# Attention and squared-ReLU feed-forward on one core: the first matrix product of chunks 3 to 6 by seven products, q of batches 2 to 7 loaded four tokens to a partition, the order of work searched anew

## The chip, the cores and the metric

The kernel runs on one core of a Trainium2 chip (trn2). The metric is device time in microseconds (us). The kernel before took 331.17 us, the median of three runs from 329.81 to 331.58. The engines are named as in the profile: PE multiplies matrices (PEld is its weight load), DVE, ACT and POOL work on vectors, SP and POOL issue most DMA transfers. PE writes its results to PSUM, eight banks of 512 fp32 numbers per partition; the others read them from there into SBUF.

## The reference

Causal attention with 16 extra "beacon" keys in front, for 8 batches of 8 heads, 576 tokens and 64 numbers per head, and then a feed-forward layer over all 4608 tokens:

```python
k_all = np.concatenate([beacon_k, k], axis=2)      # 592 keys, 5 tiles of up to 128
v_all = np.concatenate([beacon_v, v], axis=2)
scores = scale * np.matmul(q, k_all.transpose(0, 1, 3, 2))
scores = np.where(causal, -1e9, scores)            # beacons are always seen
a = softmax(scores)
attn = np.matmul(a, v_all)                         # [8, 8, 576, 64]
x = attn.transpose(0, 2, 1, 3).reshape(4608, 512)
h = x @ w_in                                       # 512 -> 2048, the first product
out = np.maximum(h, 0) ** 2 @ w_out                # 2048 -> 512, the second product
```

## The kernel before

**Order.** Every piece of work is a named operation on one engine, and a long word list (`SEQUENCE`, line 16) gives the order in which they are issued. `Order.run` (line 182) walks the list; `@A`, `@D`, `@P` after a name choose ACT, DVE or POOL where there is a choice. Each engine works its own instructions strictly in that order and waits by semaphores for what it needs. PSUM is handed out as two "strips" of two banks (scores) and four single banks `ps`.

**Attention.** Heads go in pairs, four pairs to a batch. `add_load` (line 370) reads 128 tokens of all heads into an fp32 staging tile: token on the partition, so each DMA row is one head of one token, 256 bytes. A cast (POOL, recorded at line 342 like every copy on DVE or POOL; line 340 on ACT) turns it to bf16 into `qb`/`kb`, of which there are two each, used in turn. `add_trans` (line 414, DMA at line 418) transposes a whole batch of q or k by DMA, so that `qT` and `kT` hold head dimension on partitions and tokens side by side. Batches 0 and 1 come in another way and are turned on PE (lines 474 and 476). `score_mm` (line 623, matmul at line 631) multiplies a 128-key tile by a stretch of q for each of the two heads of a pair; the two sit on partitions 0 to 63 and 64 to 127. A pair needs 1664 score columns, which are cut into the segments

```python
SEGS = [(0, 0, 240), (0, 368, 576), (1, 112, 576), (2, 240, 576), (3, 368, 576), (4, 496, 576), (0, 240, 368)]
```

(key tile, first token, last token). `add_stream` (line 663) lays the four pairs of a batch side by side, 13 banks of 512 columns, in visits of two or three. ACT takes the exponentials (line 729), DVE clips the diagonal tiles with a mask (line 750), PE multiplies by v (line 771, called av below), DVE divides (lines 788 and 790). The result goes transposed into `xT`, a ring of three batches (1728 tokens), by DMA (line 822) or PE (line 839).

In batch 0 the first 240 tokens are loaded two to a partition. There q stands in `qT` with all even tokens first and then all odd ones, 120 apart, and `score_mm` reads it with a step:

```python
rhs = qT[0][hp, pr, 0:parts_of[0][1][0]].rearrange("p (s n) -> p n s", s=ns)[:, t0 // ns:t1 // ns]
```

**Feed-forward.** 4608 tokens are nine chunks of 512. In chunks 0 to 6 the first product (`add_chunk`, line 1047, matmuls at line 1073) makes 16 tiles of 128 features, four matmuls of 512 columns each; where the ring wraps inside a chunk (chunks 3 and 6) each is cut in two. Per tile one pass over PSUM on ACT (line 1088) or DVE (line 1090) applies the ReLU, and one pass per two tiles squares in place (lines 1098, 1100).

The second product of chunks 2 to 8, and the first of chunks 7 and 8 (`BOTH = 7`), use seven products of half-size blocks in place of eight (Winograd's form). Sums of blocks are made beforehand: of `w_out` (line 882), of the squared g (line 1154, four per half chunk on DVE, in `sum_area`), of `w_in` (`add_a_sums`, line 890) and of x (line 930). In PSUM the products are added up in three chains: chain x takes products 1, 6, 7 and 4 one after the other into the same bank, and after each of the first three ACT or DVE copies the running sum out ("hold") before the next may be added; chains y (5, 3) and z (2) are read out with a held sum added ("plus", line 997). In chunks 7 and 8 (`add_first_both`, line 903, matmuls at line 950) chain x lies in the strips, which attention no longer needs, x is first copied ("pulled") into four contiguous blocks by POOL, and ReLU and squares are passes of their own (lines 1021 to 1029). `product` at line 1174 (matmuls at line 1182) is the second product's.

Of the kernel before, what the change touches and what calls it, by code (L numbers as in the profile page):

```python
# [12 lines left out]
BIG = 3.0e38  # L13
# [3 lines left out]
ident tri fldq0 fldk2 fldq1 bkl0 fldq2 fldk1 warm sld0k1.0 fldk0 sld0q1.0 fcq0 sld0k1.2 tp0.0.0q eq0.0.0@D sld0q1.2  # L17
fck2 tpg0.0.0q fck3 tp0.0.2k fcq1 ld0v0 bkc0 tp0.0.3k ek0.0.2@A ek0.0.3@D tpg0.0.2k tpb0 tpg0.0.3k tp0.0.1q ekb0
fcq3@A fcq2@D ld0v1 bkl1 eq0.0.1@A tp0.0.3q fck1 tpg0.0.1q tp0.0.2q ld0v2 eq0.0.3@A eq0.0.2@D qk3.0.0 tpg0.0.3q ld0v3
tpg0.0.2q tp0.0.1k tp0.1.0k exp3.0.0 fck0 ld0v4 qk2.0.0 ek0.0.1@D ek0.1.0@D tpg0.0.1k tp0.0.0k exp2.0.0 win0 qk1.0.0  # L20
mask3.0.0 tpg0.1.0k tp0.1.0q ek0.0.0@A mask2.0.0 exp1.0.0 qk0.0.0 tpg0.0.0k win2 tp0.1.2k eq0.1.0@A mask1.0.0 exp0.0.0
ek0.1.2@D qk0.1.0 tpg0.1.0q tp0.1.1q tpg0.1.2k win1 exp0.1.0 mask0.0.0 qk0.1.1 cast0v0@D tp0.1.1k exp0.1.1 eq0.1.1@D
qk0.1.2 mask0.1.1 win3 tpg0.1.1q tp0.1.2q ek0.1.1@A cast0v1@D exp0.1.2 eq0.1.2@D qk1.1.0 tpg0.1.1k bkc1 av0.0.0
tpg0.1.2q av1.0.0 sld1k0.0 exp1.1.0 mask0.1.0 tp0.1.3k norm0.0.0 qk2.1.0 cast0v2 tpb1 ek0.1.3@D qk1.1.1 exp2.1.0 ekb1
cast0v3 av2.0.0 norm1.0.0 tpg0.1.3k xtp0.0.0 exp1.1.1 tp0.1.3q xte0.0.0@D qk1.1.2 sld1q0.0 eq0.1.3@D xtp0.0.1 av3.0.0
exp1.1.2 norm2.0.0 tpg0.1.3q qk3.1.0 cast0v4 norm3.0.0 xtp0.0.2 exp3.1.0 sld1k0.2 qk2.1.1 mask1.1.0 av0.1.0 mask1.1.1
mask2.1.1 exp2.1.1 sld1q0.2 mask3.1.1 av1.1.0 xte0.0.1@A norm0.1.0 ld1v0 xte0.0.2@A xtp0.0.3 mask2.1.0 qk2.1.2
xte0.0.3@A norm1.1.0 xtp0.1.0 exp2.1.2 s1.0.1.0 xte0.1.0@D s1.0.3.0 relu0.1.0@D qk3.1.1 ld1v1 relu0.3.0@A s1.0.11.0
exp3.1.1 av2.1.0 relu0.11.0@D mask3.1.0 xtp0.1.1 s1.0.0.0 norm2.1.0 xte0.1.1@A s1.0.2.0 relu0.0.0@D qk3.1.2 ld1v2
relu0.2.0@A sq0.0.0@D xtp0.1.2 sq0.1.0@A s1.0.6.0 xte0.1.2@D exp3.1.2 s1.0.8.0 relu0.6.0@D s1.0.9.0 relu0.8.0@D  # L30
s1.0.10.0 relu0.9.0@A av3.1.0 sq0.4.0@D relu0.10.0@A ld1v3 sq0.5.0@D s1.0.12.0 norm3.1.0 s1.0.4.0 relu0.12.0@A
s1.0.5.0 relu0.4.0@A ld1v4 tp1.0.0k relu0.5.0@A xtp0.1.3 sq0.2.0@A ek1.0.0 s1.0.13.0 s1.0.14.0 xte0.1.3@A relu0.13.0@D
wout0 tpg1.0.0k tp1.0.0q relu0.14.0@A sq0.6.0@D s1.0.11.1 eq1.0.0@D tp1.0.1k relu0.11.1@A s1.0.8.1 wout1 tpg1.0.0q
ek1.0.1 tp1.0.1q relu0.8.1@A qk4.2 tpg1.0.1k eq1.0.1@D tp1.0.2k wout2 exp4.2.0.0.0 s1.0.15.1 tpg1.0.1q ek1.0.2
tp1.0.3q exp4.2.1.0.0 s1.0.12.1 wout3 tpg1.0.2k eq1.0.3@D s1.0.5.1 relu0.12.1@A mask4.0.0 qk4.4 tpg1.0.3q relu0.15.1@A
relu0.5.1@D cast1v0 s1.0.2.1 exp4.4.0.0.0 tp1.0.2q cast1v1 relu0.2.1@D s1.0.14.1 eq1.0.2@D exp4.4.1.0.0 cast1v2
s1.0.13.1 relu0.14.1@D s1.0.0.1 tpg1.0.2q relu0.13.1@A cast1v3 mask4.0.2 mask4.0.1 qk5.7 sq0.7.1@A sq0.6.1@D cast1v4
# [105 lines left out]
s2.8.1.0 sum8.4.1 sum8.2.0 s2.8.5.0 ev8.c1.0@A sum8.3.0 s2.8.1.1 sum8.4.0 s2.8.6.0 ev8.c1.1@A s2.8.5.1 ev8.u2.0@D  # L143
ev8.c11.None s2.8.7.0 st8.0.0.0 s2.8.6.1 st8.0.1.0 ev8.u3.0@A ev8.c22.0 s2.8.4.0 ev8.u2.1@A s2.8.7.1 ev8.c21.0@A
st8.1.0.0 s2.8.3.0 ev8.u3.1@A ev8.c22.1 s2.8.4.1 ev8.c12.0 st8.0.0.256 s2.8.3.1 ev8.c21.1@A st8.1.1.0 ev8.c12.1
st8.0.1.256
"""


# [1188 lines left out]
```

## Time and profile before

| | us |
|---|---|
| median of three runs | 331.17 (329.81 to 331.58) |
| span of the profiled execution, first to last instruction | 327.7 |
| busy PE / DVE / ACT / POOL | 315.9 / 231.9 / 225.7 / 101.1 |
| granted PE clock, mean | 1.000 |

The profile gives one execution. The span leaves out what lies before the first and after the last instruction: 331.17 − 327.7, some 3.5 us, if that execution was like the median run. A row of a group of instructions reads: line, engine, operation, output<-input with its shape, count | busy us, mean ns of one | idle us of the engine just before them, and what ended it. A row of the timeline reads: start, length in us, engine, line, operation, count. In a table of stretches each engine's busy us stand with the count of its instructions, then the granted PE clock, the DMA share and GB/s.

### The profile page before, as it was taken

Reading aid. Unit: us, or ns where it says so; the run is one execution under the profiler, and the core shown is the slowest. Engines: PE = TensorE matmul, PEld = TensorE weight load, DVE = VectorE, ACT = ScalarE, POOL = GpSimd, SP = SyncE. Lnnn points to the kernel's source line nnn. Section 1 sums busy time; section 2 is a strip of 40 time slices with the busy share of each in tenths; the row PEclk is TensorE's granted clock in tenths of the full one; section 3 lists DMA queues with packets and bytes.
Section 4 is the critical chain, followed back from the end, with each engine's and each line's share of the span. In section 5 each row is a group of like instructions: output and inputs, shape, how many; then the busy total and the mean of one; then the engine's idle time right before and its main releaser. Section 6 shows DMA issues by size and latency. Waiting matters only on the chain.

```text
span 327.7 us, 8732 instructions
## 1 busy us (share of the span) xinstructions
PE 315.9 (96%) x3582; PEld 227.6 (69%) x3582; DVE 231.9 (71%) x487; ACT 225.7 (69%) x332; POOL 101.1 (31%) x149
## 2 busy tenths in 40 slices
PE   2999999999999999999999999999999999999995
PEld 1478785544565558888866565776788788888884
DVE  3777886534655899587864788768865797897871
ACT  4867796458874984777766889767837664695931
POOL 9854713404532450424033403641100252000000
PEclk9999999999999999999999999999999999999999
DMA  8999998899999999999999998997913210110033
GB/s 159 220 205 215 206 169 170 168 214 204 205 177 201 240 219 171 178 244 230 180 138 215 221 181 204 202 207 156 225 23 130 46 28 2 69 61 0 2 148 111
DMA packets 145602, 51.98 MB, mean 159 GB/s; under 512 B 132506, under 2 KB 140570, under 8 KB 145562
## 3 DMA queue, kind: packets, MB, share of 16 engines
q1 hardware_dynamic: 135901, 42.32, 65.7%
q0 software_dynamic: 8512, 8.49, 15.4%
q10 hardware_dynamic: 1149, 0.62, 0.9%
q8 instruction: 28, 0.46, 0.6%
q14 instruction: 12, 0.10, 0.1%
HBM read 37.22 MB, written 9.44 MB: 142 GB/s over the span
## 4 chain that ended last, share of the span: by engine, by line
PE 85%; DMA 8%; SPq 1%; ACT 1%; POOL 1%; DVE 1%; issue 1%; ACTq 0%; POOLq 0%; DVEq 0%
PE ps L1073 26%; PE ps L1182 21%; PE ps L771 9%; PE ps L1123 8%; PE strip L631 6%; PE strip L950 4%; PE ps L950 3%; DMA stg<-in_q_dram 3%; PE strip L1182 2%; DMA kT<-qk_area 2%; PE ps L631 2%; DMA osb<-in_q_dram 2%; DMA stg<-in_v_dram 2%; PE ps L839 1%; SPq L822 1%; PE ps L474 1%
## 5 line engine op out<-in xcount | busy, mean ns | idle before, releaser
L1073 PE MATMUL ps<-xT,w_in 128*128 128x512 bf16 (+6 forms) x640 | 106.3, 315 | 0.6 <-ACT pt L729 0.6
L1073 PEld LDWEIGHTS <-w_in 128*128 128x128 bf16 x640 | 56.2, 98 | 34.8 <-issue 1.6
L729 ACT ACTIVATE pt<-strip 128x1024 bf16<-128x1024 f32 (+3 forms) x77 | 69.6, 955 | 7.8 <-PE strip L631 7.7
L1088 ACT ACTIVATE g<-ps 128x512 bf16<-128x512 f32 (+2 forms) x82 | 44.4, 551 | 20.1 <-PE ps L1073 17.2
L342 POOL CAST qk_area<-stg 128x512 bf16<-128x512 f32 (+2 forms) x60 | 39.9, 672 | 53.7 <-DMA stg<-in_k_dram 31.5
L342 POOL CAST vb<-stg 128x512 bf16<-128x512 f32 (+1 forms) x38 | 27.4, 728 | 83.6 <-DMA stg<-in_v_dram 69.4
L750 DVE TENSOR_TENSOR pt<-pt,tri 128x512 bf16<-128x512 bf16 (+1 forms) x93 | 37.8, 424 | 16.1 <-ACT pt L729 14.8
L1182 PEld LDWEIGHTS <-g 128*128 128x128 bf16 x448 | 42.9, 98 | 7.0 <-issue 0.8
L771 PEld LDWEIGHTS <-pt 128*128 128x128 bf16 x930 | 35.8, 100 | 7.0 <-issue 1.2
L771 PE MATMUL ps<-vb,pt 128*128 128x65 bf16 x930 | 38.4, 197 | 0.0
L1182 PE MATMUL ps<-w_out,g 128*128 128x256 bf16 x304 | 38.0, 273 | 0.0
L1090 DVE TENSOR_SCALAR g<-ps 128x512 bf16<-128x512 f32 (+2 forms) x46 | 27.9, 607 | 13.2 <-PE ps L1073 12.6
L1182 PEld LDWEIGHTS <-sum_area 128*128 128x128 bf16 x336 | 32.0, 98 | 5.5 <-issue 1.4
L790 DVE TENSOR_TENSOR xn<-ps,rcp 128x320 bf16<-128x320 f32 (+2 forms) x64 | 31.5, 491 | 2.2
L340 ACT COPY osb<-ps 128x512 f32<-128x512 f32 x26 | 15.2, 586 | 25.2 <-PE ps L1182 19.0
L1123 PE MATMUL ps<-w_out,g 128*128 128x512 bf16 x128 | 31.2, 379 | 0.0
L1100 DVE TENSOR_TENSOR g<-g 128x1024 bf16<-128x1024 bf16 (+2 forms) x35 | 23.4, 673 | 10.6 <-ACT g L1088 9.9
L631 PEld LDWEIGHTS <-kT 64*128 64x128 bf16 x618 | 20.0, 95 | 14.1 <-issue 10.3
L631 PE MATMUL strip<-qT,kT 64*128 64x128 bf16 (+14 forms) x500 | 29.5, 246 | 0.3 <-ACT qT L340 0.2
L1098 ACT ACTIVATE g<-g 128x1024 bf16<-128x1024 bf16 (+2 forms) x29 | 26.7, 941 | 3.0 <-DVE g L1090 2.0
L729 ACT ACTIVATE pt<-ps 128x512 bf16<-128x512 f32 x42 | 23.4, 599 | 5.7 <-PE ps L631 5.6
L1182 PE MATMUL ps<-w_sum,sum_area 128*128 128x256 bf16 x208 | 26.0, 273 | 0.0
(93 smaller groups left out, 357.7 us busy)
## 6 DMA issues: line engine op xcount, KB each, us to landing
out_dram<-osb SPq DMA_DIRECT2D x16, 512.0 KB, 3.8
stg<-in_q_dram SPq DMA_DIRECT2D x24, 256.0 KB, 4.6
stg<-in_k_dram SPq DMA_DIRECT2D x18, 256.0 KB, 5.1
stg<-in_v_dram SPq DMA_DIRECT2D x18, 256.0 KB, 4.6
w_in<-in_moe_w_in_dram POOLq DMA_DIRECT2D x4, 512.0 KB, 12.0
w_out<-in_moe_w_out_dram POOLq DMA_DIRECT2D x4, 512.0 KB, 10.9
stg<-in_v_dram POOLq DMA_DIRECT2D x6, 256.0 KB, 8.0
stg<-in_k_dram SPq DMA_DIRECT2D x6, 224.0 KB, 4.1
```

Source lines behind the costliest of these rows:

```text
L342: eng[e].tensor_copy(dst, src)
L631: nc.tensor.matmul(out, kT[b % 2][hp, pr, 128 * c:128 * c + 128], rhs, start=True, stop=True)
L729: nc.scalar.activation(out, in_, AF.Exp, bias=0.0, scale=scale)
L750: nc.vector.tensor_tensor(out=d, in0=d, in1=tri[0:rows, m0:m0 + m, 0:w][:, None].to_broadcast([rows, 2, m, w]), op=ALU.min)
L771: nc.tensor.matmul(a[:, at + (t - tl[0]) * (D + 1):at + (t - tl[0] + 1) * (D + 1)], P[0:rr, hj, o:o + 128], vb[b % 2][0:rr, c, 2 * pr + hj ...
L790: nc.vector.tensor_tensor(out=xn[b % 2].rearrange("p t (h d) -> p h t d", d=D)[:, h0:h0 + nh, tl[0]:tl[0] + nt], in0=a[:, :, :, 0:D], in1= ...
L1073: nc.tensor.matmul(h[:, lo - spans[0][0]:hi - spans[0][0]], w_in_sb[:, mc, ft * 128:(ft + 1) * 128], xT[:, mc, lo % RING:lo % RING + hi - lo],
L1088: nc.scalar.activation(dst, h, AF.Relu, bias=0.0, scale=1.0)
L1090: nc.vector.tensor_scalar(out=dst, in0=h, scalar1=0.0, scalar2=None, op0=ALU.max)
L1098: nc.scalar.activation(d, d, AF.Square, bias=0.0, scale=1.0)
L1123: nc.tensor.matmul(o, G[:, fc, ts * 128:(ts + 1) * 128], w_out_sb[:, fc, :], start=(fc == 0), stop=(fc == NFT - 1))
L1182: nc.tensor.matmul(o, lhs[:, f, t * 128:(t + 1) * 128], rhs[:, f], start=fresh and f == 0, stop=f == HF - 1, skip_group_check=True)
```

## The change

**First product.** `BOTH` becomes 3: chunks 3 to 8 all make the first product by seven products, in four units per chunk (4 of the 16 feature tiles each, two of the upper and two of the lower half), every chain in one `ps` bank. Blocks of x are no longer copied: products 1, 2, 3 and 7 read them in the ring, every second token (a step of two bf16 numbers); only the sums s1, s2 and s4 are separate tiles, and a fourth sum is written back into the ring. "Plus" becomes one custom DVE instruction that adds and clips at zero, so the ReLU has no pass of its own. Per chunk: 12 holds, 4 last passes of chain x, 12 plus, 8 squares, 4 sums of x.

**q.** For batches 2 to 7 a load takes two heads and 512 tokens, four tokens to a partition: DMA rows of 1024 bytes. After the transpose token 4n+s stands at 128s+n, and `score_mm` reads q with a step of 128 numbers (four tokens, then the next number). Tokens 512 to 575 are loaded as before, so a segment that reaches past 512 becomes two matmuls.

**Room and engines.** `qb` and `kb` are single; the other half of their area holds the sums of `w_in`. Casts may run on ACT, DVE or POOL, masks and sums of g on DVE or POOL (POOL masks with two `affine_select`). Two sums of g are made in place, after products 1 and 2. The word list is new throughout: 55 of 96 masks and 20 of 56 sums of g are on POOL, 19 casts of batches 0 to 7 on ACT, 20 on DVE (2 before) and 61 on POOL. Of the 96 holds and last passes of chain x, 70 are on ACT and 26 on DVE; the 72 plus are on DVE.

```diff
-    FAST, FAST_PE = 2, 0.9
-    BOTH = 7
-    NSTG, NPT, RB = 6, 3, 3
+    FAST, BOTH = 2, 3
+    NSTG, NPT, RB, NH = 6, 3, 3, 3
...
+        fours = x == "q" and c < HP
...
+            if fours:
+                return [queue.dma_start(out=st[0:rows].rearrange("p (u s) d -> p u s d", s=4),
+                                        in_=t[b, 2 * c:2 * c + 2, 0:4 * rows, :].rearrange("u (p s) d -> p u s d", s=4))]
...
         if x != "v":
-            if b < NPE + 2:
-                deps += [zero_ops[b]]
-            else:
-                deps += trans[b - 2, x]
-        engs = ("POOL", "DVE") if b == 0 and c <= 1 else ("POOL",)
+            deps += [zero_ops[b]] if b == NPE else trans[b - 1, x]
...
     def score_mm(b, pr, st, c, t0, t1, at):
...
+            if b >= NPE:
+                fours = qT[b % 2][hp, pr, 0:512].rearrange("p (s n) -> p n s", s=4)
+                parts = [(x, y, z) for x, y, z in ((t0, min(t1, 512), fours), (max(t0, 512), t1, None)) if x < y]
+            for x, y, view in parts:
+                out = st[hj][:, at + x - t0:at + y - t0]
+                if view is None:
+                    rhs = qT[b % 2][hp, pr, x:y]
+                else:
+                    ns = view.shape[2]
+                    out, rhs = out.rearrange("p (n s) -> p n s", s=ns), view[:, x // ns:y // ns]
+                nc.tensor.matmul(out, kT[b % 2][hp, pr, 128 * c:128 * c + 128], rhs, start=True, stop=True)
...
+        def in_ring(c, q):
+            return [xT[:, HM * c:HM * c + HM, lo % RING:lo % RING + hi - lo].rearrange("p m (i q) -> p m q i", q=2)[:, :, q]
+                    for lo, hi in spans]
...
+            product(2, "z", A[0, 1], b21, cuts, feeds + weights)
+            product(1, "x", A[0, 0], b11, cuts, feeds + weights)
+            hold("c1", 1)
+            plus("c11", "z", 2, block(0, 0), "c1", True)
+            product(5, "y", a_sum[1], [s[1]], one, a_ops[1] + x_ops[1])
+            product(6, "x", a_sum[2], [s[2]], one, a_ops[2] + x_ops[2] + ev["c1"])
+            hold("u2", 6)
+            product(7, "x", A[1, 0], b12, cuts, a_ops[3] + x_ops[3] + ev["u2"])
+            hold("u3", 7)
+            plus("c22", "y", 5, block(1, 1), "u3", False)
+            product(4, "x", A[1, 1], [s[4]], one, x_ops[4] + ev["u3"])
+            last("c21", 4, block(1, 0))
+            product(3, "y", a_sum[4], b22, cuts, a_ops[4] + ev["c22"])
+            plus("c12", "y", 3, block(0, 1), "u2", True)
```

591 lines of the change are left out of this document (296 added, 295 removed).

## The prediction

> **What bounds the kernel now.** I read the totals first, then who made PE wait, then two stretches: 140 to 260 us, where chunks 3 to 6 lie, and 280 to 300 us, where first products already go by seven.
>
> ```profile
> PE 315.9 (96%) x3582; PEld 227.6 (69%) x3582; DVE 231.9 (71%) x487; ACT 225.7 (69%) x332; POOL 101.1 (31%) x149
> ...
> PE ps L474 <- ACT qk_area L340: 5.8, 2, 5.3
> ...
> PE ps L1073 <- ACT pt L729: 0.6, 1, 0.6
> PE ps L631 <- DMA kT<-qk_area: 0.5, 1, 0.5
> ...
> 140.00:260.00 120.00, 118.87 (x1463) 87.06 (x1460) 87.66 (x183) 87.66 (x124) 30.68 (x45) 1.00 0.88 175
> 280.00:300.00 20.00, 20.00 (x186) 17.94 (x184) 18.13 (x34) 14.81 (x17) 0.00 (x0) 1.00 0.14 53
> ```
>
> PE works almost without a gap: 5.8 us of waiting at the start, then single waits of 0.6 and 0.5. ACT and DVE stand at 73% in the first stretch; in the second PE is full although DVE stands at 91%. So the time is PE's work, and each term below counts as it changes that work, or opens a gap in it.
>
> **What the seven products save.** A pair of rows gives a price: from one start to the next.
>
> ```profile
> 222.12 1.89 PE L1073 MATMUL ps<-xT,w_in 128*128 128x512 bf16 x8
> 223.85 1.04 PE L1182 MATMUL ps<-w_sum,sum_area 128*128 128x256 bf16 x8
> ...
> 255.62 7.15 PE L1073 MATMUL ps<-xT,w_in 128*128 128x384 bf16 x64
> 262.61 1.04 PE L1182 MATMUL ps<-w_out,g 128*128 128x256 bf16 x8
> ...
> 268.72 1.04 PE L950 MATMUL strip<-qk_area 128*128 128x256 bf16 x8
> 269.60 1.04 PE L1182 MATMUL ps<-w_sum,sum_area 128*128 128x256 bf16 x8
> ```
>
> Two plain tiles take 1.73 us, 0.865 each, so 13.84 for the 16 of chunk 4 or 5. Cut at the wrap, eight tiles take 6.99, so 13.98 for chunk 3 or 6; the cut costs 0.009 per tile, 2 ns per extra matmul. Eight matmuls of 256 columns take 0.88 at most (other such pairs 0.87, the value I use), and a chunk by seven products has 4 units x 7 products x 4 = 112 of them: 12.2 us. Chunks 3 and 6 read four of the products in two pieces, 64 more matmuls at 2 ns, 0.1. Saved: 2 x (13.84 − 12.2) + 2 x (13.98 − 12.3) = **6.6 us** (a quarter of a us either way by rounding).
>
> **What the step in scores costs.** The trace has such reads only in batch 0 (two tokens, 120 apart), each 240 + 128 = 368 columns for both heads side by side. Next to them stand plain score visits of 336 + 80 = 416 and 208 + 256 = 464 columns at the same time, and others later.
>
> ```profile
> 9.99 0.53 PE L631 MATMUL strip<-qT,kT 64*128 64x240 bf16 x4
> 10.45 0.38 PE L474 MATMUL ps<-ident,qk_area 120*128 120x120 bf16 x2
> ...
> 12.66 0.53 PE L631 MATMUL strip<-qT,kT 64*128 64x336 bf16 x4
> 13.12 0.49 PE L474 MATMUL ps<-ident,qk_area 112*64 112x112 bf16 x6
> ...
> 14.43 0.57 PE L631 MATMUL strip<-qT,kT 64*128 64x208 bf16 x4
> 14.93 0.49 PE L474 MATMUL ps<-ident,qk_area 112*64 112x112 bf16 x6
> ...
> 24.52 0.37 PE L631 MATMUL strip<-qT,kT 64*128 64x208 bf16 x4
> 24.83 0.32 PE L839 MATMUL ps<-ident,xn 128*128 128x128 bf16 x3
> ...
> 165.25 0.61 PE L631 MATMUL strip<-qT,kT 64*128 64x240 bf16 x10
> 165.80 1.92 PE L1182 MATMUL ps<-w_sum,sum_area 128*128 128x256 bf16 x16
> ...
> 176.13 0.62 PE L631 MATMUL strip<-qT,kT 64*128 64x48 bf16 x14
> 176.69 1.05 PE L1182 MATMUL ps<-w_out,sum_area 128*128 128x256 bf16 x8
> ...
> 8.00:10.00 2.00, 1.75 (x18) 0.94 (x18) 1.40 (x4) 1.17 (x3) 1.99 (x3) 1.00 1.58 193
> ```
>
> Early, 416 columns take 0.46 and 464 take 0.50: 0.83 ns per column, which would make 368 columns 0.42. With the step they took 0.46, and the other three such visits likewise: 0.04 more, about 0.1 ns per column, a pace near 0.93. From 24 us on PE runs twice as fast: 464 columns in 0.31, 1024 in 0.55, so 0.43 ns per column. (The granted clock reads 1.00 in the early stretch too; that halving is not in this column.) No stepped read falls in the fast part, so its price there is bounded. If the extra is a fixed start cost, it is 0.04 for each of 13 banks x 6 batches = 78: 3.1 us; if it shrinks with the pace, 1.6; if it is chance, 0. If instead a read that jumps at every number cannot be fed faster than about 0.93 ns, the early visits were almost fast enough not to show it, and in the fast part the pace stays there. Stepped columns: per pair 1664 less 64 for each of the five segments that end at 576, 1344; x 4 pairs x 6 batches = 32,256. With 0.91, the lower edge of what the rounding leaves, (0.91 − 0.43) x 32,256 = **15.5 us**; the upper edge, 0.97, gives 17.4. I take 15.5, the end to which the one stepped row points: an extra at half speed is what a limit in the feeding would look like, while chance would not come four times alike. So the range must reach from 0 to 17.4.
>
> [...]
>
> The cut at token 512 adds 5 x 4 x 6 = 120 pairs of matmuls. 14 matmuls for 1024 columns took 0.56 and 10 took 0.55, so 5 ns a pair: **0.6 us**.
>
> The first product's step of two numbers has no row. Ends: nothing, or the pace 0.91 for 4 products x 16 x 256 columns x 6 chunks = 98,304 columns, 47 us. I take 0, since successive numbers lie 4 bytes apart against 240 in the stepped row, nearer to the plain reads.
>
> **What ACT, DVE and POOL get.**
>
> ```profile
> L1088 ACT ACTIVATE g<-ps 128x512 bf16<-128x512 f32 x64 | 37.8, 599 | 16.9 <-PE ps L1073 14.5 <-DVE rcp L788 1.9
> L340 ACT COPY osb<-ps 128x512 f32<-128x512 f32 x26 | 15.2, 586 | 25.2 <-PE ps L1182 19.0 <-PE ps L1123 5.3 <-DMA out_dram<-osb 0.8
> ...
> L997 DVE TENSOR_TENSOR g<-ps,stg 128x512 bf16<-128x512 f32 x16 | 10.7, 684 | 3.4 <-PE ps L950 3.4
> L1154 DVE TENSOR_TENSOR g<-g 128x1024 bf16<-128x1024 bf16 x14 | 10.3, 740 | 0.0
> L750 DVE TENSOR_TENSOR pt<-pt,tri 128x512 bf16<-128x512 bf16 x62 | 29.5, 478 | 11.8 <-ACT pt L729 10.5 <-ACT pt L653 1.1
> ...
> L342 POOL CAST qk_area<-stg 128x512 bf16<-128x512 f32 x48 | 32.5, 680 | 43.8 <-DMA stg<-in_k_dram 24.6 <-DMA stg<-in_q_dram 18.8
> L327 POOL TENSOR_SCALAR_AFFINE_SELECT tri<-tri 128x128 bf16<-128x128 bf16 x4 | 1.0, 296 | 0.1
> ```
>
> A chunk had 16 passes over PSUM (0.60) and now has 28 of 0.59 to 0.68, and four sums of x (no row; at most the 0.74 of line 1154, which handles twice as many numbers without a step; I take the 0.68 of line 997, which has as many). That is 12 x 0.65 + 4 x 0.68 = 10.5 us a chunk, 42 in all. Casts add 37 x some 0.6 = 22. POOL takes away, over the whole run, 55 masks of some 0.42 (23 us) and 20 sums (15 us). Net 26 on two engines that had 175 of 240 in the first stretch: near 85%, below what DVE stood at from 280 to 300. I cost it at nothing, covered by PE's own work between a hold and the next product of its chain. Without that cover a hold (0.59) counts: 48 holds in chunks 3 to 6, 28 us. The order leaves two or three other PE pieces (1.2 to 1.3 us) between most of them, so I keep 0, with a rival below.
>
> **DMA and queues.** q's loads go from 24 x 1024 rows to 24 x 256.
>
> ```profile
> DMA  8999998899999999999999998997913210110033
> ...
> q1 hardware_dynamic: 135901, 42.32, 65.7%
> q0 software_dynamic: 8512, 8.49, 15.4%
> ```
>
> A packet took 0.657 x 16 x 327.7 / 135,901 = 25 ns on q1 (mostly 256 bytes), 95 on q0 (about 1 KB). So the loads' share goes from 24,576 x 25 / 16 = 39 us to between 10 (25 ns) and 37 (95 ns) for 6144. It lies beside PE, whose only wait for DMA was the 0.5 us, taken as gone, like the 0.6: **−1.1 us**. The single `qb` and `kb` make a batch's casts wait for the transposes before; behind a late cast stand the loads on SP, which need its staging tile, then the next scores. In the new order more than ten products lie between, so 0. The start is reordered too (the first transfer is the large one of q): bounded by the 5.8 us of waiting there, I take 0.
>
> **Sum.** 327.7 − 6.6 + 15.5 + 0.6 − 1.1 = 336.1 span, with 3.5 outside 339.6; rounded to **340 us**, against 331.2 for the median of the runs.
>
> **Rivals.** (a) *The step is free or nearly so*: PE really loses work. 331.2 − 6.6 + 0.6 − 1.1 + (0 to 3.1) = 324 to 327, with small gaps 326. For it: in batch 0 the extra is a tenth. This is the case on the other side: it decides at an extra of 0.22 ns per column (7.1 us), below which the kernel is faster. (b) *ACT and DVE now wait for loads*: POOL stood 43.8 us before 48 casts, 0.9 each; 37 casts now stand in the queues that also empty PSUM. If the step is free and 0.2 to 0.3 of each of these shows on PE, 7 to 11 us: 331 to 335. For it: `cast5q0` stands directly before a hold on ACT. Against: the loads are issued earlier. (c) *Both*: 340 + 9 = 349. (d) *The step of two numbers is slow too*: 340 + 47 = 387. Against it, 4 bytes.
>
> A sum on POOL reads two tiles from SBUF, as DVE's sums and squares do. [...]
>
> **How the numbers follow.** Chances: my case 0.50 (336 to 344), (a) 0.28, (b) 0.11, (c) 0.08, (d) 0.03. About 0.5%, 1.7 us, is what a measurement can tell from no change. Faster: (a) but for 0.02, and 0.02 of (b): 0.28. The same: 0.02 of (a), 0.05 of (b): 0.07. Slower: 0.65. The range runs from 324 to 346: it leaves out (d), most of (c) and the lowest edge of (a), some 0.15.
>
> **What would show it.** Right: a score visit of 1024 columns in batches 2 to 7 takes 0.9 to 1.0 us, not 0.55; a product of four matmuls in chunk 4 takes 0.44; PE busy grows by some 9 us with few waits. (a) shows as visits of 0.55 to 0.65; (b) as waits of PE for holds, with ACT idle on staging tiles; (d) as products of 0.8 us. I am wrong if the visits keep their length.

## The result, and the profile after

The changed kernel took 374.58 us in the median (371.87 to 376.88), the kernel before 331.27 beside it: a ratio of 1.132, 95% interval 1.126 to 1.139. The forecast was 340, the range ended at 346: the direction was foreseen, the size was not. Ratios and their intervals leave out executions in a slower state of the chip: one of six in the first kernel under "Order restored once" below and two of six in the third, whose medians and ranges hold them. The profiled execution is the slowest of its four, at 376.88 us; its span is 375.2 us against 327.7.

The page of the changed kernel: totals, granted clock over the span in 40 slices, and the largest DMA queue.

```profile
PE 356.6 (95%) x3988; PEld 254.1 (68%) x4002; DVE 253.1 (67%) x492; ACT 232.3 (62%) x353; POOL 149.7 (40%) x222
...
PEclk9999999999999999999999999989996999999999
...
q1 hardware_dynamic: 117469, 42.32, 52.4%
```

PE is busy 40.7 us longer and still fills 95%. So most of the 47.5 us is not waiting, it is matmuls that last longer. The rest shows in the waits of PE (engine, line, what it waited for: us in total, times, longest):

```profile
PE ps L826 <- DVE g L1048: 3.8, 1, 3.8
PE ps L826 <- DVE pt L806: 2.2, 1, 2.2
```

Before, no wait of PE behind the start was above 0.6. The two stalls on DVE, 3.8 and 2.2 us, are new. Which matmuls became longer is seen in the timeline (start, duration, engine, line; the price of a row is taken from its start to the next):

```profile
177.66 1.75 PE L681 MATMUL strip<-qT,kT 64*128 64x240 bf16 x14
179.34 0.72 PE L1219 MATMUL ps<-w_out,g 128*128 128x256 bf16 x5
...
211.65 0.62 PE L1010 MATMUL ps<-xT,w_in 128*128 128x256 bf16 x4
212.10 0.60 PE L1010 MATMUL ps<-spare,qk_area 128*128 128x256 bf16 x4
```

A visit of 14 score matmuls over 1024 columns, 896 of them read with the step, takes 1.68 us; before, a visit of 14 over as many columns took 0.56. The forecast had 0.9 to 1.0. A product of four matmuls with a step of two numbers takes 0.45, almost the 0.437 of one without.

A sum over the trace puts all in one table. Each matmul counts from its start to the start of the next one, but at most its own duration; what is left over is the gap. Groups by source line, us:

| | before | after | q read as stored | the same, x in halves | by tokens, x in halves |
|---|---|---|---|---|---|
| scores | 31.0 | 72.8 | 32.2 | 32.1 | 30.5 |
| first products, plain and by seven | 124.0 | 122.1 | 122.0 | 119.7 | 119.2 |
| second products | 115.4 | 114.8 | 114.0 | 115.4 | 115.5 |
| attention times v | 32.0 | 34.5 | 33.4 | 32.6 | 32.3 |
| gaps | 2.7 | 10.2 | 6.1 | 3.1 | 7.6 |

The last three columns are experiments below. In two of the traces, after and q read as stored, 14 plain matmuls have no record: that lowers both rows of products there, and about 1.1 us of their gaps lie at these places. Scores alone grew by 41.8, gaps by 7.5; the first products shrank by 1.9, where 6.6 were forecast.

The two stalls cost more than their gaps. Toward the end of each the granted clock fell to 0.50 and stayed there for some 3 and 7 us:

```profile
140.00:240.00 100.00, 99.85 (x1211) 74.31 (x1210) 71.01 (x132) 69.59 (x102) 47.49 (x82) 1.00 0.76 159
...
285.00:290.00 5.00, 4.82 (x52) 0.50 0.01 3
```

(The second line lists PE alone.) Behind the stall of 3.8 us two groups of av and one each of the second and the first product, from 285.18 to 289.49, took 4.31 us; the same four took 2.36 in the kernel "Sums off POOL" below, which hasn't this stall. Nowhere else in this execution was the clock under 0.9 for a whole us.

### The profile page after: what moved, and what is told of

It reads as the page before. It is cut to its first block, busy times and chain, and to the rows that moved or that the text cites. A ratio compares the mean times of both kernels' runs of the same rounds, so it can differ in the third digit from the quotient of the medians.

```text
span 375.2 us, 9752 instructions
## 1 busy us (share of the span) xinstructions
PE 356.6 (95%) x3988; PEld 254.1 (68%) x4002; DVE 253.1 (67%) x492; ACT 232.3 (62%) x353; POOL 149.7 (40%) x222
## 3 DMA queue, kind: packets, MB, share of 16 engines
q1 hardware_dynamic: 117469, 42.32, 52.4%
q0 software_dynamic: 8512, 8.49, 13.7%
## 4 chain that ended last, share of the span: by engine, by line
PE 87%; DVE 6%; issue 3%; DMA 2%; POOL 1%; ACT 0%; DVEq 0%; POOLq 0%
PE ps L1219 19%; PE ps L1010 18%; PE strip L681 14%; PE ps L1113 12%; PE ps L826 8%; PE ps L1162 7%; PE ps L681 4%; PE strip L1219 2%; DMA stg<-in_v_dram 2%; DVE g L1048 2%; DVE pt L806 1%; PE ps L894 1%; POOL qk_area L500 1%; DVE spare L986 1%; DVE xn L845 1%
## 5 line engine op out<-in xcount | busy, mean ns | idle before, releaser
L802 POOL TENSOR_SCALAR_AFFINE_SELECT pt<-pt 128x256 bf16<-128x256 bf16 (+1 forms) x92 | 36.6, 422 | 107.1 <-ACT pt L779 91.4
L1048 DVE CUSTOM_DVE_ANT_0 g<-ps,spare 128x512 bf16<-128x512 f32 x72 | 48.9, 687 | 23.5 <-PE ps L1010 18.1
L681 PE MATMUL strip<-qT,kT 64*128 64x128 bf16 (+14 forms) x652 | 61.8, 330 | 0.5 <-ACT qT L349 0.4
L349 ACT COPY spare<-ps 128x512 f32<-128x512 f32 x50 | 29.2, 588 | 35.1 <-PE ps L1010 34.3
L1113 PE MATMUL ps<-xT,w_in 128*128 128x512 bf16 (+2 forms) x250 | 45.6, 329 | 0.3
L1010 PE MATMUL ps<-xT,w_in 128*128 128x256 bf16 (+4 forms) x384 | 42.9, 250 | 0.5 <-DMA xT<-xn 0.5
L1074 ACT ACTIVATE g<-g 128x1024 bf16<-128x1024 bf16 x34 | 35.7, 1059 | 2.5 <-DVE g L1048 2.3
L1188 POOL TENSOR_TENSOR g<-g 128x1024 bf16<-128x1024 bf16 x14 | 31.0, 2225 | 15.6 <-DVE g L1188 11.2
L1010 PEld LDWEIGHTS <-qk_area 128*128 128x128 bf16 x320 | 27.7, 97 | 6.7 <-issue 1.5
L1010 PE MATMUL ps<-spare,qk_area 128*128 128x256 bf16 x192 | 28.7, 272 | 0.4 <-DVE spare L986 0.3
```

Of the source, the lines that this page charges most:

```text
L681: nc.tensor.matmul(out, kT[b % 2][hp, pr, 128 * c:128 * c + 128], rhs, start=True, stop=True)
L802: nc.gpsimd.affine_select(out=d[:, :, i], in_=d[:, :, i], compare_op=ALU.is_ge, fill=0.0, base=Nb if m0 + i == 0 else 0, pattern=[[0, 2], ...
L1010: nc.tensor.matmul(o[:, i * HT + at:i * HT + at + w], lhs[:, m, f * 128:(f + 1) * 128], part[:, m], start=fresh and i == 0 and at == 0 and ...
L1048: nc.vector._custom_dve(TENSOR_ADD_SAT, out=dst, in0=bank_of(chain), in1=held[keep[added].held[1]].rearrange("p (f t) -> p f t", f=2), s0= ...
L1074: nc.scalar.activation(both, both, AF.Square, bias=0.0, scale=1.0)
L1113: nc.tensor.matmul(h[:, lo - spans[0][0]:hi - spans[0][0]], w_in_sb[:, mc, ft * 128:(ft + 1) * 128], xT[:, mc, lo % RING:lo % RING + hi - lo],
```

## The experiments

Every variant of the whole kernel was timed beside the kernel before, on the same chip; its median there lay between 329.1 and 331.3. Between variants of different rounds, differences of 2 us or less are therefore read from the ratios.

**The step alone.** The kernel before, with q of batches 2 to 7 loaded by four and read by scores with the step; products and order as they were.

```diff
+        fours = x == "q" and c < HP and b >= NPE
...
+            if b >= NPE:
+                fours = qT[b % 2][hp, pr, 0:512].rearrange("p (s n) -> p n s", s=4)
+                parts = [(x, y, z) for x, y, z in ((t0, min(t1, 512), fours), (max(t0, 512), t1, None)) if x < y]
```

> The kernel before with the loads of four tokens and the stepped scores alone; seven products for chunks 7 and 8 only, order as before. Theory S: 331 + 43 = 374, within 4. Rival O: below 345.

It took 369.85 (369.63 to 370.3), ratio 1.119 (1.113 to 1.124), just under the 370 to 378 of theory S. The first line of its page:

```profile
PE 355.6 (97%) x3785; PEld 237.4 (65%) x3810; DVE 229.5 (62%) x487; ACT 228.5 (62%) x332; POOL 96.5 (26%) x149
```

PE is as busy as in the changed kernel, with almost no gaps. This one part makes nearly the whole slowdown.

**All but the step.** The changed kernel, with the loads by four and the cut at 512 kept, but q read in the order in which it is stored.

```diff
-                parts = [(x, y, z) for x, y, z in ((t0, min(t1, 512), fours), (max(t0, 512), t1, None)) if x < y]
+                parts = [(x, y, None) for x, y in ((t0, min(t1, 512)), (max(t0, 512), t1)) if x < y]
```

> The changed kernel with the loads of four tokens and the cut at token 512 kept, but q read as it is stored, without a step (the scores are of other tokens, so the output is not the reference's). Theory S: 324 to 331, and no slower than the run with q by tokens, since only the read is changed. Rival L (the loads of four tokens or their casts cost something): over 340 here while the run with q by tokens is near 330. Rival O: above 345 in both.

It took 329.54 (327.5 to 330.25), ratio 0.996 (0.993 to 0.998). The visit of 14 matmuls, and what follows it:

```profile
158.48 0.62 PE L681 MATMUL strip<-qT,kT 64*128 64x240 bf16 x14
159.03 3.67 PE L1219 MATMUL ps<-w_out,g 128*128 128x256 bf16 x32
```

The same 14 matmuls over the same columns take 0.55. The count of matmuls and the cut cost nothing that shows in this visit; the step costs 374.58 − 329.54 = 45 us in the new order. By the table 40.6 of it are the scores' own; this kernel also has neither of the two stalls.

**The loads alone, in the old order.** The step-alone kernel without its step, on the kernel before.

> The kernel before with q of batches 2 to 7 loaded four tokens to a partition and cut at 512, but read as stored, without a step (scores are of other tokens, the work is the same). Beside the kernel before at 331.3. If the loads and casts cost nothing by themselves, only the cut is left, 120 pairs of cut matmuls by some 5 ns: 331.3 to 332.3. If the loads by four ease a wait in the old order: under 330.5. If the casts of 128 rows by 1024 numbers hold up ScalarE or VectorE: over 333.

It took 329.59 (328.39 to 330.46), ratio 0.998 (0.996 to 1.000): a gain of some 0.8, in which the cost of the cut is contained. So the step costs 369.85 − 329.59 = 40.3 us in the old order. And against 329.54 above, the seven products, the new engines and the new order bring nothing in sum. That is a second question, taken up below.

**q by tokens.** The changed kernel with q loaded and read as before: no step, no cut.

```diff
-        fours = x == "q" and c < HP
+        fours = False
...
-            if b >= NPE:
+            if False:
```

> The changed kernel with q of batches 2 to 7 loaded and read as before (128 tokens to a load, no step, no cut at token 512); seven products and the new order stay. Theory S (the step in the scores costs nearly all of it: 30 visits, each 1.1 to 1.6 us longer than before): visits of 1024 columns take 0.55 us again and the time falls by some 43 us from 374.6, to 326 to 333. Rival O (the new order and the seven products cost most of it, by waits): the time stays above 345.

It took 333.91 (332.42 to 336.56), ratio 1.010 (1.007 to 1.014), just above the 326 to 333 of theory S. In the new order the loads by tokens cost 4.4 us against the loads by four: among PE's waits stands one of 2.4 us for the transposed k.

**The price of a read.** Matmuls alone, 16 for each pattern, one behind another. L47 reads 512 neighbouring numbers, L50 every second one, L53 every fourth, L59 every sixteenth; L62 takes 2 x 120 numbers from two places 120 apart in turn (the pattern of batch 0), L71 4 x 128 from four places in turn (the new scores), L74 4 x 120; L86 the same four places with two neighbours each time, L89 with four.

> Not the reference's computation: 16 matmuls each with the moving operand read in 16 patterns, the price of a column from start to start. If any jump at each number costs the same (theory J): 2 x 120, 2 x 128, 4 x 120, 4 x 136 and 4 x 128 all take about 1.7 ns per column, pairs half of that. If the distance matters (theory B: jumps of 256 bytes meet in one place of the memory): 4 x 128 and 2 x 128 take 1.7, while 2 x 120 and 4 x 136 take under 1.0. Steps of 2 and 4 numbers: 0.43 in both theories; 8 and 16 numbers (16 and 32 bytes) like a jump in J.

```profile
22.18 3.62 PE L47 MATMUL ps<-X,W 128*128 128x512 bf16 x15
25.63 3.78 PE L50 MATMUL ps<-X,W 128*128 128x512 bf16 x16
29.25 7.38 PE L53 MATMUL ps<-X,W 128*128 128x512 bf16 x16
36.45 2.88 PE L56 MATMUL ps<-X,W 128*128 128x512 bf16 x3
...
50.85 14.86 PE L59 MATMUL ps<-X,W 128*128 128x512 bf16 x16
65.54 3.84 PE L62 MATMUL ps<-X,W 128*128 128x240 bf16 x16
69.21 4.06 PE L65 MATMUL ps<-X,W 128*128 128x256 bf16 x16
...
80.86 13.99 PE L71 MATMUL ps<-X,W 128*128 128x512 bf16 x16
94.67 13.14 PE L74 MATMUL ps<-X,W 128*128 128x480 bf16 x16
...
149.14 7.18 PE L86 MATMUL ps<-X,W 128*128 128x512 bf16 x16
156.15 3.73 PE L89 MATMUL ps<-X,W 128*128 128x512 bf16 x16
159.72 3.62 PE L92 MATMUL ps<-X,W 128*128 128x512 bf16 x16
```

From start to start and per column (16 x 512 = 8192, for L62 3840): neighbours 0.42 ns (16 matmuls, of which the record holds 15), every second 0.44, every fourth 0.88, every sixteenth 1.79, four places in turn 1.69 (13.81 / 8192). With two neighbours at each place 0.86, with four 0.44, as good as plain. Two places in turn: 0.96 (3.67 / 3840). That the places lie 256 bytes apart doesn't matter: four places 240, 264 and 272 bytes apart cost 1.69 too. What counts is how many numbers are taken from a piece of 16 bytes before the read moves on: a step of eight numbers, 16 bytes, costs 1.76, and twice that step hardly more. Two expectations were missed: a step of four numbers should have cost 0.43, and two places as much as four, but two cost little more than half of four. And there lies the fault of the forecast: its pace of 0.93 per column from batch 0 is near what that pattern costs alone, but that is the pace for two tokens to a partition.

The granted clock is not the cause. It fell to 0.50 in the long stepped stretches of this run, but every fourth number cost its 0.88 in a stretch where it read 1.00 (18 to 36 us), and the visit of the changed kernel, at 1.00, pays the same: (1.68 − 0.55) / 896 = 1.26 ns more for each stepped column, 1.69 in all.

**Runs and offsets.** Eight matmuls of a pattern, then 24 plain ones. L53 takes every third number, L63 three runs of 160 in turn, L88 fours from four places, beginning two numbers into a piece of eight.

> Matmuls alone, eight of each pattern and 24 contiguous ones between (nothing of the reference is computed). Theory J (each move to another line of 16 bytes costs 1.7 ns, however far, unless the next number is in the same line): step of 3 numbers 0.64 ns per column (2.67 numbers in a line), step of 6 numbers 1.27, three runs of 160 and six of 80 in turn 1.69, two and four runs of 8 neighbouring numbers in turn 1.69 (the next number lies in the line beside), fours in turn 0.43 at offset 0 and at offset 4 numbers, but 0.85 at offsets 2 and 6, where a four lies over two lines; pairs in two runs 0.85. Theory K (what counts is how many runs are open: two cost 0.95, four 1.69): three runs about 1.3, six runs over 1.69, two runs of 8 neighbours 0.95, four of them 1.69, pairs in two runs about 0.48, fours at offset 2 not slower than at 0.

```profile
25.87 2.88 PE L53 MATMUL ps<-X,W 128*128 128x512 bf16 x8
28.58 5.35 PE L55 MATMUL ps<-X,W 128*128 128x512 bf16 x24
...
45.48 3.97 PE L63 MATMUL ps<-X,W 128*128 128x480 bf16 x8
49.29 5.34 PE L65 MATMUL ps<-X,W 128*128 128x512 bf16 x24
...
99.10 2.80 PE L88 MATMUL ps<-X,W 128*128 128x512 bf16 x8
101.73 5.35 PE L90 MATMUL ps<-X,W 128*128 128x512 bf16 x24
```

Every third number costs 2.71 us / 4096 = 0.66 ns (theory J 0.64); every sixth gave 1.32 (J 1.27). Fours cost 0.435 at offsets 0 and 4 and 0.64 at 2 and 6, where every second four, not every four as J's 0.85 assumed, lies over two pieces. For three runs in turn neither theory is right: 3.81 / 3840 = 0.99 (J 1.69, K 1.3). Two runs of eight neighbours gave 0.95, four 1.71; pairs from two runs 0.53, between K's 0.48 and J's 0.85. So: pieces of 16 bytes set the price, about 1.7 ns for a move to another one when four or more are visited in turn, and a little over half of it for two or three. Why two or three are cheaper stays open.

**x in contiguous halves.** The kernel that reads q as stored, and the first product by seven reads halves of a chunk in place of even and odd tokens.

```diff
-...rearrange("p m (i q) -> p m q i", q=2)[:, :, q]
+...rearrange("p m (q i) -> p m q i", q=2)[:, :, q]
```

> The kernel that reads q as stored, and beside it the first product of chunks 3 to 6 reads contiguous halves of the tokens instead of every second one (the output rows of those chunks are of other tokens; the count of matmuls and columns is the same). It stands beside 329.54. Theory T (the step of two numbers costs 4 to 5 ns on a matmul of 256 columns, 113 against 109 ns): 448 such matmuls by 4 ns are 1.8 us, so 327.2 to 328.2, and the groups of four matmuls of the first product of seven fall from 0.45 to 0.435 us. Theory W (what is missing of the saving of seven products lies in waits on the holds, not in the step): 329.0 to 330.0.

It took 325.34 (324.6 to 326.27), ratio 0.985 (0.982 to 0.988): 4.2 less, by the ratios 3.6, more than theory T's 1.8. With the step of two (first fence) and without (second), groups by line, with the mean ns of one:

```profile
L1010 PE MATMUL ps<-xT,w_in 128*128 128x256 bf16 x192 | 27.8, 275 | 1.1 <-DMA xT<-xn 0.6 <-DVE xT L986 0.5
...
L986 DVE TENSOR_TENSOR spare<-xT,spare x10: 349/680/692, 139.4 to 288.0; 128x512 bf16<-128x512 bf16 x6, 128x192 bf16<-128x192 bf16 x1, 128x320 bf16<-128x320 bf16 x1, 128x384 bf16<-128x384 bf16 x1
```

```profile
L1010 PE MATMUL ps<-xT,w_in 128*128 128x256 bf16 x192 | 27.0, 272 | 0.0
...
L986 DVE TENSOR_TENSOR spare<-xT,spare x10: 248/421/449, 138.2 to 283.4; 128x512 bf16<-128x512 bf16 x6, 128x192 bf16<-128x192 bf16 x1, 128x320 bf16<-128x320 bf16 x1, 128x384 bf16<-128x384 bf16 x1
```

A matmul gains only 3 to 4 ns; in the table above the first products gain 2.3 us. The sums of x on DVE gain more: the median falls from 0.68 to 0.42 us, and PE's waits of 1.1 us ahead of these matmuls go. The gaps fall by 3.0, of which about 1.1 are the missing records. So the step of two was paid for twice, on PE and at the start of chunks.

**Shorter holds.** The same kernel that reads q as stored, each hold copying half of its bank.

```diff
-                    copy_on(e, held[box["op"].held[1]], ps[bank["x"].held[1]])
+                    copy_on(e, held[box["op"].held[1]][:, 0:256], ps[bank["x"].held[1]][:, 0:256])
```

> The kernel that reads q as stored, and beside it every hold of a finished product copies 256 columns of the bank instead of 512 (the later sums of chunks 3 to 6 then add stale values in half their columns). Theory W (the matmuls of the first product wait some tenths of a us at a time for a hold that frees their bank): the copies are about half as long, the small waits before these matmuls shrink from 7.6 us in sum by 2 or more, and the time falls from 329.54 to 326.5 to 328. Theory T (the matmuls themselves are longer): 329.0 to 330.0.

It took 335.07 (333.69 to 336.09): 5.5 more, where neither theory allowed it. ACT's holds did fall, from 590 to 375 ns. But a stall had appeared that the same kernel with whole holds hasn't:

```profile
215.86 4.80 DVE L806 TENSOR_TENSOR pt<-pt,tri 80x160 bf16<-80x160 bf16 x1
...
216.38 4.18 POOL L1188 TENSOR_TENSOR g<-g 128x1024 bf16<-128x1024 bf16 x2
...
221.32 0.98 PE L826 MATMUL ps<-vb,pt 128*128 128x65 bf16 x15 [4.26 <-DVE g L1048]
```

Of five masks on DVE the last, which takes 0.23 us where nothing holds it, starts while POOL still makes a cast (215.61 to 216.41 us) and ends only with the two sums that follow it; the pass over a bank behind it is late, and PE waits 4.26 us. The order of instructions is the same; only the times at which they meet have moved. Whether the holds cost PE anything can't be read from this run.

**The same stall in the changed kernel, and alone.** The 3.8 us of the changed kernel:

```profile
277.88 6.56 DVE L351 CAST vb<-stg 80x512 bf16<-80x512 f32 x1
...
279.97 4.19 POOL L1188 TENSOR_TENSOR g<-g 128x1024 bf16<-128x1024 bf16 x2
...
284.36 0.68 DVE L1048 CUSTOM_DVE_ANT_0 g<-ps,spare 128x512 bf16<-128x512 f32 x1
...
285.18 0.98 PE L826 MATMUL ps<-vb,pt 128*128 128x65 bf16 x15 [3.84 <-DVE g L1048]
285.98 1.90 PE L1219 MATMUL ps<-w_out,g 128*128 128x256 bf16 x8
287.67 1.03 PE L826 MATMUL ps<-vb,pt 128*128 128x65 bf16 x15
```

A cast that takes 0.4 elsewhere takes 6.56 and ends with POOL's sums. It stands from 277.88 us on, though, when POOL has just begun three selects of a mask; two casts follow there, and the sums start only at 279.97. (The last two lines show the lowered clock: the eight matmuls take 1.69 us to the next start, elsewhere 0.87.) To see the sums' part without the rest, DVE and POOL alone:

> VectorE instructions alone and beside GpSimd instructions (nothing of the reference is computed): GpSimd runs 4 sums of 128x1024 or 10 casts of 128x512, and VectorE 12 instructions of one kind at the same time, first with two SBUF inputs (256 and 512 columns), then casts from SBUF, then copies from a bank, then a bank plus SBUF. Theory L: the kinds that read SBUF alone stand while a GpSimd sum runs (one of them takes 2 us or more), the copies from a bank go on at 0.69 us and so does the bank plus SBUF. Otherwise: every kind goes on, longer by at most a half.

```profile
7.86 0.23 DVE L38 TENSOR_TENSOR K<-C,D 128x256 bf16<-128x256 bf16 x1
8.00 0.68 DVE L44 COPY T<-S 128x512 f32<-128x512 f32 x1
8.02 6.51 POOL L50 TENSOR_TENSOR P<-A,M 128x1024 bf16<-128x1024 bf16 x3 [7.58 <-DVE M L54]
8.60 1.69 DVE L38 TENSOR_TENSOR K<-C,D 128x256 bf16<-128x256 bf16 x1
```

Alone, the DVE instruction with two SBUF inputs takes 0.23; beside POOL's sum it takes 1.69, until that sum (2.2 us) is over. The copy from a bank keeps its 0.68. Casts from SBUF took 1.74 beside a sum and 0.41 without. Beside POOL's casts nothing was slowed (0.28, 0.41). A bank plus SBUF kept its 0.68. For sums, theory L holds but for its "2 us or more"; POOL's selects were not in this run.

**Sums off POOL.** The changed kernel with all sums ahead of the second product on DVE: in the word list `@P` becomes `@D` at 20 places.

> The changed kernel with all sums ahead of the second product on VectorE (0.95 us each), none on GpSimd (2.2 us). Theory L (a VectorE instruction that takes its inputs from SBUF and comes beside such a GpSimd sum stands until that sum has ended, as the masks that took 3.68 us and the cast that took 6.56 us did): the two waits of TensorE of 3.8 and 2.2 us go, VectorE gets 20 sums of 0.95 us more, the time falls from 374.6 by 3 to 6. If these two stalls had another cause, a load or a queue: within 2 us of 374.6, or slower by the added VectorE work.

It took 372.76 (372.12 to 374.0), ratio 1.130 (1.126 to 1.135) against 1.132 (1.126 to 1.139): no gain that can be told from none, where 3 to 6 us were expected. The two stalls are gone from PE's waits, but others stand there (for DVE's sums 1.9, for the sums of x 1.6), and the gaps fall only from 10.2 to 9.8. So on DVE the sums seem to cost about what the stalls had. And the cast of the longer stall, at its place in the order, still stands:

```profile
272.90 2.39 DVE L351 CAST vb<-stg 80x512 bf16<-80x512 f32 x1
```

No sum is on POOL here. It makes the same three selects and two casts, from 272.85 to 275.00 us, and the cast ends behind them, just in time for PE. So sums are not the whole of it: a DVE instruction from SBUF can stand beside a row of other POOL work too, though POOL's casts alone held up nobody in the run above. Which of POOL's instructions it needs stays open.

**The step in the bank.** q is read in runs of neighbours, and the product is written to every fourth place of the bank.

```diff
-                    out, rhs = out.rearrange("p (n s) -> p n s", s=ns), view[:, x // ns:y // ns]
+                    out = out.rearrange("p (n s) -> p s n", s=ns)
+                    rhs = view.rearrange("p n s -> p s n")[:, :, x // ns:y // ns]
```

> The changed kernel with the same scores, but q is read in runs of neighbouring numbers (one run for each of the four tokens of a partition, after each other) and the step is put where the product is written: every fourth fp32 of the bank, 16 bytes apart. Theory R (only the read of the operand pays for a move to another line of 16 bytes): the visit of 1024 columns falls from 1.68 to 0.55 to 0.6 us and the time to that of the kernel that reads q as stored, 329.5, at most 332. Theory S (a step of 16 bytes costs as much where it is written as where it is read, 1.7 ns for each number): near 370 again.

It took 351.01 (349.52 to 352.51), ratio 1.064 (1.060 to 1.068): between the theories. The visit of 14 matmuls:

```profile
162.53 0.99 PE L682 MATMUL strip<-qT,kT 64*128 64x240 bf16 x14
163.45 3.67 PE L1220 MATMUL ps<-w_out,g 128*128 128x256 bf16 x32
```

0.92 us, 0.37 more than the 0.55 of the kernel that reads q as stored: 0.41 ns more for each of the 896 columns with the step, so about 0.84, twice the 0.43 of a plain write and half of the stepped read. Of the 21.5 us by which this kernel is slower than the one that reads q as stored, 13.5 are scores; the two stalls came back here, with 4.2 and 3.8 us.

**That, with x in halves.** Cuts at the ring's wrap within a half, hidden values and stored rows in the order of tokens.

```diff
-            return [xT[:, HM * c:HM * c + HM, lo % RING:lo % RING + hi - lo].rearrange("p m (i q) -> p m q i", q=2)[:, :, q]
+            return [xT[:, HM * c:HM * c + HM, (t0 + q * HT + at) % RING:(t0 + q * HT + at) % RING + w] for at, w in cuts]
...
-                nc.sync.dma_start(out=out[t0:t1, :].rearrange("(t p q) d -> q p t d", q=2, t=2)[v], in_=osb[v])
+                nc.sync.dma_start(out=out[t0:t1, :].rearrange("(q t p) d -> q p t d", q=2, t=2)[v], in_=osb[v])
```

> As the kernel that puts the step in the bank, and beside it the four parts of x are contiguous halves of a chunk's tokens instead of even and odd tokens (the hidden values and the stored rows follow, so that the same is computed). If the written step is free and the step of two is worth what the kernel without it gave (4.2 us): 325 to 326. If the written step costs: 4 us below the kernel that puts the step in the bank.

347.38 (346.17 to 348.51): 3.6 below, near the 4 expected.

**Halves, q by tokens.** The same halves in the kernel that loads q by tokens.

> Seven products in halves and the new order alone: q loaded by tokens as before (333.9 with even and odd tokens). If the step of two in x was worth the 4.2 us of the kernels that read q as stored: 329.5 to 330.5. If these 4.2 us came from waits that the loads by tokens bring back: 332 to 334.

It took 328.71 (326.14 to 329.96), ratio 0.995 (0.992 to 0.998), 5.2 below the kernel by tokens with even and odd tokens. Of the versions in which scores and stored rows are of their own tokens it is the only one that beats both kernels: the kernel before by 0.5%, with an interval from 0.2 to 0.8.

```profile
PE 309.7 (95%) x3774; PEld 239.6 (74%) x3774; DVE 239.5 (74%) x492; ACT 228.5 (70%) x353; POOL 151.5 (47%) x222
...
PE ps L681 <- DMA kT<-qk_area: 1.9, 1, 1.9
...
PE strip L681 <- DMA kT<-qk_area: 1.2, 2, 1.0
```

PE is busy 6.2 us less than before (315.9), so the work of seven products is indeed saved. The first products make 4.8 of it in the table. But the gaps are 7.6 against 2.7: the saving meets waits for k of 3.1 us, of which the order of the kernel before had 0.5.

**Order restored once.** A transposed q put back into token order by copies, after which scores read neighbours; x in halves. First with pairs 0 and 2 on DVE, 1 and 3 on POOL, then the same with the sums on DVE.

```diff
+            def emit_order(e, pr=pr):
+                copy_on(e, qT[0][:, pr, 0:512].rearrange("p (n s) -> p n s", s=4),
+                        qT[1][:, pr, 0:512].rearrange("p (s n) -> p n s", s=4))
+                copy_on(e, qT[0][:, pr, 512:S], qT[1][:, pr, 512:S])
```

> The kernel with halves, but q is put back into the order of its tokens once, by one copy for each pair of heads (pairs 0 and 2 on VectorE, 1 and 3 on GpSimd) ahead of the scores, which then read neighbouring numbers; the transposed q goes through the second buffer. Without the step the same work with other tokens gave 325.3. Theory H (the loads by four, the seven products in halves and the new order are worth 4 us together once nobody steps through q on TensorE): 24 copies of some 1 us lie on engines with idle time: 325 to 328.5. Rival (the copies, or scores that wait for them, or VectorE standing beside GpSimd's sums, eat the gain): 329 or more.

> As the kernel with the order restored, all sums ahead of the second product on VectorE. If VectorE stands beside GpSimd's sums in that kernel (waits of TensorE of about 4 us for a VectorE instruction, as in the kernels with the step in the bank): 2 to 6 us less. If not: 0 to 2 us more, by VectorE's 20 sums of 0.95 us.

342.52 (341.38 to 346.61), ratio 1.039 (1.035 to 1.043), and 344.33 (342.22 to 346.82), ratio 1.044 (1.039 to 1.049): the rival held, and moving the sums gave nothing. The waits of PE in the first of them:

```profile
PE ps L834 <- DVE xn L853: 5.0, 4, 4.0
PE ps L1017 <- DVE g L1055: 4.6, 2, 2.6
PE strip L689 <- DVE qT L353: 2.3, 1, 2.3
```

The copies are no work for PE, but PE waits for the norms and the passes over banks that stand in DVE's queue with them, and for one copy. Two more put the copies elsewhere: all on POOL, or on ACT (pairs 0 and 3) and POOL.

> The kernel with the order restored, all copies on GpSimd (0.79 us on average for each of 48, as in the kernel with the order restored), put right behind the transposes in the order, VectorE left alone. If the 342.5 came from VectorE's share (its copies ahead of the norms and of the passes over the hidden values, for which TensorE waited 10 us): 327 to 332. If it came from the copies wherever they lie (scores that wait for them): 338 or more.

> The same with pairs 0 and 3 copied by ScalarE, 1 and 2 by GpSimd, 14 places ahead of the first scores. If only VectorE was the trouble: 327 to 334, with ScalarE's exponentials somewhat later. If the copies hold up the scores on any engine: 338 or more.

347.1 (344.44 to 351.33), ratio 1.050 (1.046 to 1.055), and 330.31 (328.51 to 331.69), ratio 1.003 (1.000 to 1.005). The waits of the first show why it was worse, a miss of its expectation for "only DVE":

```profile
PE ps L834 <- POOL pt L810: 13.7, 4, 4.6
...
L353 POOL COPY qT<-qT 128x512 bf16<-128x512 bf16 (+1 forms) x48 | 32.5, 723 | 14.5 <-DMA qT<-qk_area 13.3 <-PE ps L1017 1.2
```

POOL stands 13.3 us before copies whose q has not landed; behind them in its queue are masks, and PE waits 13.7 for those. With ACT and POOL, later in the order, PE waits 4.8 us for holds on ACT, and what the loads by four gain is spent. The two kernels make the same copies and differ by some 16 us: it is a matter of the queues they stand in and of their place in the order, not of the copies alone.

## Why the prediction was wrong, step by step

**PE bounds the kernel**: right. With the step alone PE is 97% busy and the time is PE's.

**The step in scores, 15.5 us, range 0 to 17.4**: here the forecast failed. It gave such a read a pace of its own ("a read that jumps at every number cannot be fed faster"), and it failed at "in the fast part the pace stays there". The 0.93 ns of batch 0 hold for two tokens to a partition; measured alone this pattern gives 0.96. That the reading came so near is in part luck: it rests on 0.04 us between rounded rows of whole visits, which end with some 0.2 us to the next line that hide the step. Matmul by matmul the trace before had more than "a tenth": at the same time 240 stepped columns stand 0.24 us, as long as 336 plain ones (0.23). Four tokens cost 1.69. With it the forecast's own sum is (1.69 − 0.43) x 32,256 = 40.6 us, and the step alone cost 40.3 in the old order. Neither end of the range was a bound: a row of another pattern bounds nothing unless one knows what the pattern changes. The visit forecast at 0.9 to 1.0 us is what the step written to the bank gave, by coincidence.

One number from a piece of 16 bytes before the next piece (four places in turn, or a step of eight or sixteen numbers) cost 1.69 to 1.79 ns in the runs of matmuls alone, against 0.42 for neighbours. Two numbers from a piece cost 0.86 to 0.88 each, and only four came near plain, 0.44.

**Seven products, −6.6**: the mechanism is right, the term mis-sized. By tokens and in halves PE's first products shrink by 4.8 us and PE's busy time by 6.2. The price of a matmul was right: of 544 whole matmuls of 256 columns 511 take 109 ns or little more, as forecast. The other 33 stand longer before the next one starts, and make 2.0 us; before, none of 224 did. So the part that is missing is small waits that count as matmul time; for what, the trace does not show. As made, with even and odd tokens, 1.9 were left.

**The step of two, 0 (bound 47)**: near 0 on PE, 3 to 4 ns a matmul, but not 0: 4.2 us of the time with the slower sums of x on DVE. By the ratios it is 3.6. The forecast looked only at the matmuls, not at DVE, which reads the same step (0.68 us for a sum of x with it, 0.42 without).

**The cut, 0.6**: scores took 0.9 to 1.2 us more with it (31.9 in the old order and 32.2, against 31.0).

**ACT, DVE and POOL, 0**: not covered as argued. It was averaged as busy time, and what came was DVE and POOL instructions meeting: 3.8 + 2.2 us in the changed kernel, and at a granted clock of 0.50 some 2 us more behind the longer one alone. It took no late loads, as (b) has them, to cost 3.8 us at once. In the kernel that reads q as stored the two don't meet, so this is a risk of the timing and not a fixed price.

**DMA, −1.1**: the packets of q1 fell by 18,432, as counted (135,901 − 117,469). Together with the cut, −0.5 was forecast and −0.8 measured, with an interval from −1.4 to 0.

**Rivals**: (a), the step free, decides at an extra of 0.22 ns a column; it was 1.26. Its time, 326, is what the kernel without either step gave, 325.3. (b) came in half: the stall of 3.8 us is a cast that stands in DVE's queue ahead of a pass over PSUM, but it stood beside POOL's work, not for a load. (d) named the wrong step; that its 387 lies nearer to 374.58 than the forecast does is luck.

The sum by measured terms: 327.7 − 1.9 (first products) + 41.8 (scores) + 7.5 (gaps) + 2.5 (attention times v) gives 377.6; the start and the other matmuls, each a little shorter, bring it to the span of 375.2. About 1.5 of the 2.5 stand behind the two stalls, at the lowered clock.

## What to carry to other kernels

Before a layout is turned to make a load cheaper, ask who reads it next, number by number: here a matmul's moving operand cost 0.44 ns a column with four numbers of two bytes from each 16, near the plain 0.42, 0.88 with two and 1.76 to 1.79, four times the plain price, with one. A row for a similar access is not a bound; say what differs and what it would cost if the price grew with it. When POOL gets elementwise work, look at which DVE instructions from SBUF can fall beside it (1.69 us in place of 0.23 beside a sum here), and who waits behind them.

## What the runs showed of the hardware

- The price of a stepped read by piece: 0.42 ns a column for eight numbers of a piece of 16 bytes, 0.44 for four, 0.66 for 2.7, 0.88 for two, 1.32 for 1.3, 1.76 to 1.79 for one. Two or three places in turn, one number each, cost 0.95 to 0.99; four and more 1.68 to 1.85.
- A bank written at every fourth fp32 costs about 0.84 ns a column, an estimate from 0.37 us more for 896 such columns.
- In the runs of matmuls alone the granted clock fell during stepped stretches (0.50 from 107 to 135 us of the first) and the plain matmuls behind them were slower: 24 took 5.18 us as a rule, 6.33 behind every sixth number and 7.05 to 7.42 behind six or four places in turn. In the changed kernel the clock stayed at 1.00 from 140 to 240 us, and a stepped column cost the same, 1.69 ns.
- Behind stalls of PE of 2.2 and 3.8 us in the changed kernel the granted clock read 0.50 for some 3 and 7 us, and what ran there took up to twice as long: 1.69 us in place of 0.87 for eight matmuls. In eight of the 16 whole kernels PE waited 2.2 us or more at once behind the start, up to 4.6; each of these has slices of a granted clock under 0.9 on its page. Of the other eight, with waits of at most 2.0, one has such a slice, the kernel with the copies on ACT and POOL.
- DVE and POOL alone: a DVE instruction with its inputs in SBUF stood until POOL's sum ended, 1.69 us in place of 0.23; copies from a bank kept their 0.68, and beside POOL's casts these instructions took 0.28 and casts on DVE 0.41, against 0.23 to 0.28 and 0.36 to 0.41 without. In the kernel with the sums off POOL a DVE cast stood 2.39 us beside three selects and two casts.
